# Attention scores of five groups in four 64x64 tiles over two PSUM banks, with a newly computed instruction order

## The chip, the cores and the metric

The kernel runs on one core of one Trainium2 chip. The metric is the device time of one execution in microseconds (us). Three runs of the kernel before gave 615.8, 616.06 and 616.22, so the median is 616.06 us.

## The reference

The reference chains three layers over 1152 tokens (2 batches of 576) of width 512 (8 heads of 64):

```python
scores = scale * np.matmul(q, k.transpose(0, 1, 3, 2))       # scale = 1/8
mask_local = (rel >= 0) & (rel < 32)                         # heads 0 to 3
mask_strided = (rel >= 0) & (pos[None, :] % 32 == pos[:, None] % 32)   # heads 4 to 7
attn = exp(scores - max) / (sum + 1e-09)
x = attn @ v                                                 # 1152 x 512
h = np.maximum(x @ w_in, 0.0); x = (h * h) @ w_out           # d_ff 2048
out += p[:, e:e+1] * (np.maximum(x @ w1[e], 0) @ w2[e])      # 4 experts of 1024, p = normalised domain_probs
```

All inputs are fp32.

## The kernel before, in words

**Attention.** Only the unmasked parts of the score matrix are computed, in 16 groups. A `Local` group is a window of queries of heads 0 to 3 (64 queries against 96 keys for a unit), a `Strided` group is a set of residues modulo 32 of heads 4 to 7 (54 or 36 rows for a unit). `attend` (L518 on) adds the steps of one group: three loads (k, q, v), the scores on TensorE (`scores`, L417 and L488), the mask, the row maximum on VectorE (`L556`), exp on ScalarE (`L561` or `L567`), the sum, the normalisation (`L571`), the transposes on TensorE (`L430`, `L501`), a copy to SBUF (`pt`, `L540`/`L542`), the product with v on TensorE (`L442`, `L511`) and the split of its result into a rounded and a rest part (`hi` `L582`/`L584`, `lo` `L588`). The scores are fp32 products of 64x64 tiles: head 0 of a unit uses array rows 0 to 63 and output partitions 0 to 63, head 1 rows 64 to 127 and partitions 64 to 127, all into one PSUM bank `S`. Each product is recorded in the trace as two matmuls (two passes).

The mask of -8e9 is added in one of two ways, group by group (`ON_PE`, for the ten groups after the first six). With 1, TensorE multiplies an identity by the mask first (`L421`, `L492`) and the scores accumulate on it. With 0, VectorE adds the mask while it copies the scores to SBUF (`L549`).

**First layer pair.** `run_steps` multiplies x by w_in (`H` in the banks `bh`, L774 to L776: three products for each split fp32 one), squares the ReLU (relu `L839` on ScalarE, square `L843` on VectorE, then `L846` and `L849` split the result into `h`), and multiplies by w_out two steps later (`by<-h,w`, also L774 to L776). The weights are loaded as 8-byte words, decoded (`L734`, `L737`, `L742`) and split (`L749`/`L751` and `L755`). From about 100 us on the same work goes through Strassen's scheme, and from about 250 us on the experts follow in a scheme of fifteen products.

**What sets the order.** Every step is a task of the class `Plan` with a cost in ns on each engine that may run it, a rank, PSUM or SBUF buffers that it takes and gives back, and the tasks that it follows. `Plan.run` plays the tasks through an event queue: an idle engine gets the ready task of the lowest rank whose buffers are free. The instructions are then emitted in that order, engine by engine, and the chip keeps it. Ranks and lead times are a table of numbers (`START` to `T_LEAD1`). Until the first product of the first layer is planned, an idle TensorE gets a filler product into a spare bank (`L1455`, 512 columns).

Of the kernel before, what the change touches and what calls it, by code (L numbers as in the profile page):

```python
# [68 lines left out]
class Plan:  # L69
# [33 lines left out]

    def run(self):
# [21 lines left out]
        while done < len(self.tasks):  # L126
# [25 lines left out]
            for e in ready:  # L152
                while idle[e] and ready[e]:
                    held, got = [], None
                    while ready[e]:
# [4 lines left out]
                        if not (t.quiet and e in self.tense or (t.port or e == "pool") and now < self.shared) and all(any(self.rings[r] for r in rings) for _, _, rings in t.take):  # L160
                            got = t
                            break
# [12 lines left out]
                    got.end = now + got.engines[e] * (2 if e == "pe" and now < self.warm else 1)  # L175
# [19 lines left out]
def tile_attention_mlp_experts(ctx: ExitStack, tc: tile.TileContext, a, out):  # L195
# [24 lines left out]
    HOLD = 4828  # L220
    AHEAD = 9478
    END2 = 25419
    END3 = -2590
    CONV = 19315
    CONV1 = 64257
    CONV2 = -317
# [3 lines left out]
    R_MASK = 1005  # L230
    ON_PE = (1, 1, 1, 1, 0, 0, 0, 0, 0, 0)
    FILL = 0
    R_MAX = -1769
    R_EXP = -5627
    R_NORM = 2220
# [3 lines left out]
    R_LO = -53571  # L239
    R_OUT = 2681  # L240
    FIRST = (-22394, 16695, 607, 23035, 8563, 1593)
    WHOLE = (1, 1, 1, 0, 0, 0)
    S_T, S_V, S_X = -14699, 658, 1170
    L_T, L_V, L_X = 4928, -8176, -46841
    LKQ = (-8725, -8905, -8392, -8132, -7820, -7895)
    LV = (-8661, -8282, -6737, -7657, -6434, -5679)
    LW = {("wi", 0, 1): -8036, ("wi", 0, 0): -7136, ("wi", 1, 1): -5574, ("wo", 0, 0): -7535, ("wo", 0, 1): -7891, ("wi", 1, 0): -6538}
    EARLY = {("wi", 0, 1): -35560, ("wi", 0, 0): 15804, ("wi", 1, 1): 33114, ("wo", 0, 0): 44988, ("wo", 0, 1): -1604, ("wi", 1, 0): 21441}
    GROUP = 4
    AHEAD_H = 3  # L250
    EARLY_H = (8793, 10693, 10315, 12215), (-10835, -8935, 44549, 46449), (8730, 10630, 20923, 22823), (19925, 21825, 13108, 15008)
# [7 lines left out]
    LEAD = 3482  # L259
    L_CB = -10608  # L260
    L_ID = -8381
    WI1 = 1
# [4 lines left out]
    S_LEAD = -14791  # L267
    S_LEAD1 = 75203
    T_LEAD1 = 28673
# [114 lines left out]
    class Strided:  # L384
# [32 lines left out]
        def scores(self, env, masked):  # L417
            self.views(env)
            n, s = self.n, env["S"]
            if masked:  # L420
                nc.tensor.matmul(s[:, : U * n], lhsT=cmat("ident", P), rhs=spread(cmat(self.R, P), U), start=True, stop=False)  # L421
            for u in range(U):
                for h in range(2):
                    hd = slice(h * D, (h + 1) * D)
                    nc.tensor.matmul(s[h * D : h * D + n, u * n : (u + 1) * n], lhsT=env["q3"][hd, u, :], rhs=env["k3"][hd, u, :], start=not masked, stop=not masked or u == U - 1)
# [9 lines left out]
        def values(self, env):  # L435
            n = self.n
            for h in range(2):
                for g in range(GROUPS):
                    c, q = (h * GROUPS + g) * n, g * P + h * D
                    for k in range(2):  # L440
                        rows = slice(k * D, k * D + n)
# [13 lines left out]
    class Local:  # L455
# [32 lines left out]
        def scores(self, env, masked):  # L488
            self.views(env)
            units, s = self.units, env["S"]  # L490
            for key, u, v in self.masks() if masked else ():
                nc.tensor.matmul(s[:, u * WIN : v * WIN], lhsT=cmat("ident", P), rhs=spread(cmat(key, P), v - u), start=u == 0, stop=False)  # L492
            for u in range(units):
                j, t = divmod(u, 2)
                for h in range(2):
                    hd = slice(h * D, (h + 1) * D)
                    nc.tensor.matmul(s[hd, u * WIN : (u + 1) * WIN], lhsT=env["q3"][hd, u, :], rhs=env["k3"][hd, t, j * WQ : j * WQ + WIN], start=not masked, stop=not masked or u == units - 1)  # L497
# [8 lines left out]
        def values(self, env):  # L506
            for u in range(self.units):
                for h in range(2):
                    j, t = divmod(u, 2)
                    c = t * self.nq + j * WQ  # L510
                    nc.tensor.matmul(env["X"][h * D : (h + 1) * D, c : c + WQ], lhsT=env["v3"][:, 4 * j + 2 * t + h, :], rhs=env["pt"][:WIN, u * P + h * WQ : u * P + (h + 1) * WQ], start=True, stop=True)  # L511
# [8 lines left out]
    def attend(g, rank, rings, lead, early=None, whole=False, on_pe_=1):  # L520
# [24 lines left out]
        t = plan.add({"pe": g.cost_s - (0 if masked else mm_r(n))}, lambda e: g.scores(env, masked), after=[t_cb, t_go, *loads[:2], *(transposed[-3:-2] if len(rings) == 1 else [])], rank=rank, take=[(env, "S", rings)], free=[(env, "q"), (env, "k")])  # L545
# [363 lines left out]
    def strassen(t_in, left, right, ready, w_free, s_free, rank_pe):  # L909
# [17 lines left out]
        def at(key):  # L927
            return c[key][:, :TB]
# [616 lines left out]
```

## Time and profile before

| | before |
|---|---|
| median of three runs | 616.06 us |
| the profiled execution, its own time | 616.26 us |
| its span (first to last instruction) | 614.3 us |
| TensorE matmul busy | 608.9 us, 99% |
| VectorE / ScalarE / GpSimdE busy | 455.9 / 300.7 / 133.0 us |
| last matmul ends, last VectorE instruction begins | 610.96, 610.99 us |

The span is 1.96 us less than the profiled execution's time; what lies around the span is launch and end. A timeline row has the start, the length, the engine, the line, the operation, the tiles written and read, the shapes and the count; where rows of one line follow each other they are merged. Lengths of matmuls overlap, so the cost of a piece is read from its start to the start of the next piece.

### The profile page before, as it was taken

The numbers are of one execution on the slowest core, as the hardware profiler recorded it, in microseconds if no ns is written. First come the engines' busy times: TensorE is split into PE (matmuls) and PEld (weight loads), VectorE is DVE, ScalarE is ACT, GpSimd is POOL, SyncE is SP. The second block draws the span as 40 slices with busy tenths as digits, with TensorE's granted clock in tenths as the row PEclk, the third lists the DMA queues.
The fourth block names the chain that finished last, engine by engine and source line by source line (L and its number), as shares of the span: only waits on it lengthen the run. The fifth ranks groups of instructions, "written<-read, shape, count | busy, mean of one in ns | idle before, by whom it ended". The sixth has DMA issues, their size and how long they took to land.

```text
span 614.3 us, 10072 instructions
## 1 busy us (share of the span) xinstructions
PE 608.9 (99%) x3739; PEld 558.5 (91%) x3739; DVE 455.9 (74%) x899; ACT 300.7 (49%) x698; POOL 133.0 (22%) x156
## 2 busy tenths in 40 slices
PE   9999999999999999999999999999999999999997
PEld 5798999999999999998898989898998989898996
DVE  5798868984797984977666675868866676987654
ACT  3778774755464653665344544334344534344330
POOL 3422113500010201032032232313141322224000
PEclk9999999999999999999999999999999999999999
DMA  8987422232313100030110203020201202020012
GB/s 262 303 252 229 125 83 70 68 96 77 103 52 87 36 0 18 1 86 18 38 49 18 86 19 86 18 86 17 65 22 32 74 17 86 18 86 1 1 52 102
DMA packets 37440, 45.13 MB, mean 73 GB/s; under 512 B 4688, under 2 KB 26640, under 8 KB 37392
## 3 DMA queue, kind: packets, MB, share of 16 engines
q1 hardware_dynamic: 37392, 44.50, 24.4%
q8 instruction: 29, 0.48, 0.3%
q14 instruction: 19, 0.16, 0.1%
HBM read 42.13 MB, written 2.36 MB: 72 GB/s over the span
## 4 chain that ended last, share of the span: by engine, by line
PE 96%; DMA 2%; DVE 0%; SPq 0%; ACT 0%; issue 0%; ACTq 0%
PE bh L774 12%; PE bh L776 12%; PE bh L775 12%; PE by L1307 11%; PE by L1306 11%; PE by L1308 11%; PE by L774 5%; PE by L776 5%; PE by L775 5%; PE ba L774 4%; PE ba L776 4%; PE ba L775 3%; DMA raw<-in_wi_dram 1%; PE ba L497 1%; DMA q<-in_qs_dram 1%; PE ba L511 1%
## 5 line engine op out<-in xcount | busy, mean ns | idle before, releaser
L1259 DVE SCALAR_TENSOR_TENSOR acc<-by,pe,acc 128x512 f32<-128x512 f32 (+1 forms) x109 | 79.3, 742 | 24.3 <-PE by L1308 24.0
L774 PE MATMUL bh<-x,w 128*128 128x384 f32 x234 | 80.5, 344 | 0.0
L776 PE MATMUL bh<-x,w 128*128 128x384 f32 x234 | 78.4, 335 | 0.0
L775 PE MATMUL bh<-x,w 128*128 128x384 f32 x234 | 78.4, 335 | 0.0
L1204 POOL TENSOR_TENSOR sf<-raw,raw 128x256 f32<-128x256 f32 x40 | 32.3, 816 | 185.9 <-DMA raw<-in_w_dram 108.0
L1215 ACT ACTIVATE w<-sf 128x256 fp32r<-128x256 f32 x110 | 42.0, 406 | 35.8 <-POOL sf L1204 35.8
L1307 PE MATMUL by<-o,h 128*128 128x512 f32 (+1 forms) x134 | 52.3, 390 | 0.0
L1306 PE MATMUL by<-o,h 128*128 128x512 f32 (+1 forms) x134 | 52.0, 388 | 0.0
L1308 PE MATMUL by<-o,h 128*128 128x512 f32 (+1 forms) x134 | 51.7, 386 | 0.0
L774 PE MATMUL by<-h,w 128*128 128x384 f32 x152 | 51.4, 338 | 0.0
L776 PE MATMUL by<-h,w 128*128 128x384 f32 x152 | 50.8, 335 | 0.0
L775 PE MATMUL by<-h,w 128*128 128x384 f32 x152 | 50.8, 334 | 0.0
L774 PEld LDWEIGHTS bh<-x,w 128*128 128x128 f32 x234 | 43.9, 188 | 2.4 <-DVE r L1426 1.1
L775 PEld LDWEIGHTS bh<-x,w 128*128 128x128 f32 x234 | 44.0, 188 | 0.4
L776 PEld LDWEIGHTS bh<-x,w 128*128 128x128 f32 x234 | 43.9, 188 | 0.0
L1328 ACT ACTIVATE h<-r 128x384 fp32r<-128x384 f32 x26 | 13.7, 525 | 53.5 <-DVE r L1426 53.5
L1204 POOL TENSOR_TENSOR sf<-sf,raw 128x256 f32<-128x256 f32 x40 | 32.1, 813 | 29.0 <-DVE w L1223 28.9
L775 PE MATMUL bh<-w,w 128*128 128x384 f32 x110 | 36.9, 336 | 0.0
L776 PE MATMUL bh<-w,w 128*128 128x384 f32 x110 | 36.9, 335 | 0.0
L1426 DVE TENSOR_TENSOR r<-r,bh 128x384 f32<-128x384 f32 x50 | 27.5, 550 | 12.6 <-ACT r L1421 7.9
L774 PE MATMUL bh<-w,w 128*128 128x384 f32 x110 | 36.8, 335 | 0.0
L1236 ACT ACTIVATE o<-raw 128x512 fp32r<-128x512 f32 x30 | 18.8, 631 | 35.1 <-PE by L1308 34.7
(282 smaller groups left out, 1615.6 us busy)
## 6 DMA issues: line engine op xcount, KB each, us to landing
raw<-in_wi_dram SPq DMA_DIRECT2D x16, 512.0 KB, 4.2
raw<-in_wo_dram SPq DMA_DIRECT2D x16, 512.0 KB, 4.5
raw<-in_w_dram SPq DMA_DIRECT2D x64, 128.0 KB, 2.7
raw<-in_w_dram SPq DMA_DIRECT2D x32, 256.0 KB, 2.8
out_dram<-acc SPq DMA_DIRECT2D x8, 256.0 KB, 2.0
v<-in_vs_dram SPq DMA_DIRECT2D x6, 256.0 KB, 5.1
v<-in_vl_dram SPq DMA_DIRECT2D x8, 192.0 KB, 5.6
k<-in_kl_dram SPq DMA_DIRECT2D x8, 160.0 KB, 4.6
```

What stands on the lines that cost most here:

```text
L774: nc.tensor.matmul(dst, lhsT=wh, rhs=xh, start=start, stop=False, skip_group_check=again)
L775: nc.tensor.matmul(dst, lhsT=wh, rhs=xl, start=False, stop=False, skip_group_check=again)
L776: nc.tensor.matmul(dst, lhsT=wl, rhs=xh, start=False, stop=stop, skip_group_check=again)
L1204: nc.gpsimd.tensor_tensor(out=value(dst), in0=value(x), in1=value(y), op=ALU.subtract if n in MINUS else ALU.add)
L1215: nc.scalar.activation(out=op_slot(env["op"])[:, 0].rearrange("p k f -> p (k f)"), in_=value(src), func=AF.Copy, scale=float(sign))
L1236: nc.scalar.activation(out=late[env["w2"]][:, 0], in_=f32(raws[f]["raw"][:, DM:]), func=AF.Copy)
L1259: nc.vector.scalar_tensor_tensor(out=acc, in0=o, scalar=pcol, in1=acc, op0=ALU.mult, op1=ALU.add)
L1306: nc.tensor.matmul(o, lhsT=h[:, 0, ts], rhs=w[:, 0], start=new, stop=False)
L1307: nc.tensor.matmul(o, lhsT=h[:, 0, ts], rhs=w[:, 1], start=False, stop=False)
L1308: nc.tensor.matmul(o, lhsT=h[:, 1, ts], rhs=w[:, 0], start=False, stop=stop)
L1328: nc.scalar.activation(out=got(env["hid"])[:, 0], in_=src(), func=AF.Relu)
L1426: nc.vector.tensor_tensor(out=at_(), in0=at_(), in1=bank["bank"][:, :TB], op=ALU.add if sign > 0 else ALU.subtract)
```

## The change

1. **Scores.** For groups with the mask on VectorE, the scores go to four tiles over two banks: unit u writes bank `S0` or `S1` by u modulo 2, and in odd units the two heads change places in the output partitions. So four neighbouring products have four different 64x64 tiles. The product with v reads its columns accordingly (`turned`). The second bank may be one of the pair `bank_h`, as may the one of the product with v (`HB`).
2. **Planned cost.** These scores are planned with 0.62 of the cost (`QUAD`). The planner checks that two buffers taken together are both free (`fits`), and it stretches or shortens planned DMA time by three factors.
3. **Mask and scale.** VectorE multiplies by the scale while it adds the mask, in one instruction for each bank and mask; the maximum comes out negated, so the later multiplication by -scale falls away for these groups.
4. **Which groups.** `ON_PE` goes from 1111000000 to 1110001001: five groups with the mask on VectorE instead of six.
5. **Squares.** In the first layer the square of a step may run on ScalarE (`SQ`). In the order that results, 21 of 32 do.
6. **The table.** Nearly every number of the table has another value, so the whole order of the first 250 us is another one.

```diff
-                        if not (...) and all(any(self.rings[r] for r in rings) for _, _, rings in t.take):
+                        if not (...) and self.fits(t):
...
-                    got.end = now + got.engines[e] * (2 if e == "pe" and now < self.warm else 1)
+                    slow = 2 if e == "pe" and now < self.warm else 1
+                    if e == "dma":
+                        slow = 1.25 if now < 5000 else 0.83 if now < 6700 else 1
+                    got.end = now + int(got.engines[e] * slow)
...
-    HOLD = 4828
+    HOLD = 5337
-    ON_PE = (1, 1, 1, 1, 0, 0, 0, 0, 0, 0)
+    SQ = (0, 50, 0)
+    QUAD = 0.62
+    HB = (1, 0, 1)
+    ON_PE = (1, 1, 1, 0, 0, 0, 1, 0, 0, 1)
...
                 for h in range(2):
-                    hd = slice(h * D, (h + 1) * D)
-                    nc.tensor.matmul(s[h * D : h * D + n, u * n : (u + 1) * n], lhsT=env["q3"][hd, u, :], ...)
+                    hd, c, y = slice(h * D, (h + 1) * D), h * D, s[:, u * n : (u + 1) * n]
+                    if not masked:
+                        c, y = (h + u) % 2 * D, env["S%d" % (u % 2)][:, u // 2 * n : (u // 2 + 1) * n]
+                    nc.tensor.matmul(y[c : c + n], lhsT=env["q3"][hd, u, :], ...)
...
+        more = rings if masked or not HB[0] else rings + ["bank_h"]
+        held = [(env, "S")] if masked else [(env, "S0"), (env, "S1")]
-        t = plan.add({"pe": g.cost_s - (0 if masked else mm_r(n))}, ..., take=[(env, "S", rings)], ...)
+        t = plan.add({"pe": g.cost_s if masked else int((g.cost_s - mm_r(n)) * QUAD)}, ..., take=[(x, y, rings if k == 0 else more) for k, (x, y) in enumerate(held)], ...)
...
-                    nc.vector.tensor_tensor(out=view(env["p"])[:, u:v], in0=view(env["S"], g.cols)[:, u:v], in1=spread(cmat(key, P), v - u), op=ALU.add)
+                    for k in range(2):
+                        x = env["S%d" % k][:, u // 2 * g.cols : v // 2 * g.cols].rearrange("p (u c) -> p u c", c=g.cols)
+                        nc.vector.scalar_tensor_tensor(out=pairs[:, k, u // 2 : v // 2], in0=x, scalar=SCALE, in1=spread(cmat(key, P), (v - u) // 2), op0=ALU.mult, op1=ALU.add)
...
-                    nc.vector.scalar_tensor_tensor(out=h, in0=h, scalar=0.0, in1=env["r"], op0=ALU.max, op1=ALU.mult)
+                    if e == "act":
+                        nc.scalar.activation(out=h, in_=env["r"], func=AF.Square, scale=WSCALE**0.5)
+                    else:
+                        nc.vector.scalar_tensor_tensor(out=h, in0=h, scalar=0.0, in1=env["r"], op0=ALU.max, op1=ALU.mult)
```

The order on TensorE, at the scores of a Strided group with 54 rows (k and q are its inputs, `ba` and `bh` PSUM banks, cb the mask). Before:

```order
L421 LDWEIGHTS cb
L421 MATMUL ba_106<-cb 128x432
L425 MATMUL ba_106<-k_116,q_112 54x54 x16
L442 MATMUL ba_105<-pt_130,v_122 64x54 x16
L774 MATMUL by_107<-h_97,w_82 128x384
```

Now, the group that follows it:

```order
L442 MATMUL ba_106<-k_115,q_111 54x54 x2
L442 MATMUL bh_104<-k_115,q_111 54x54 x2
L442 MATMUL ba_106<-k_115,q_111 54x54 x2
L442 MATMUL bh_104<-k_115,q_111 54x54 x2
L442 MATMUL ba_106<-k_115,q_111 54x54 x2
L442 MATMUL bh_104<-k_115,q_111 54x54 x2
L442 MATMUL ba_106<-k_115,q_111 54x54 x2
L442 MATMUL bh_104<-k_115,q_111 54x54 x2
L800 MATMUL by_107<-h_97,w_81 128x384
```

The mask product is gone for this group, and two banks alternate. It also shows that the first output product (`by_107<-h_97`) has moved: it follows this group's scores directly.

The order on TensorE, ahead of the first product of the first layer (`bh_103<-x_75,w_80`). Before:

```order
L501 MATMUL by_107<-ident,p_129 96x128 x4
L501 MATMUL ba_106<-ident,p_128 96x128 x4
L1455 LDWEIGHTS idle
L1455 MATMUL by_110<-idle 128x512
L1455 LDWEIGHTS idle
L1455 MATMUL by_110<-idle 128x512
L774 MATMUL bh_103<-x_75,w_80 128x384
```

Now:

```order
L459 MATMUL by_109<-pt_131,v_119 64x54 x16
L459 MATMUL ba_105<-pt_130,v_121 64x36 x16
L520 MATMUL ba_106<-ident,p_129 96x128 x4
L530 MATMUL by_107<-pt_131,v_123 64x64 x8
L800 MATMUL bh_103<-x_75,w_80 128x384
```

A product with v of a Local group now stands ahead of it, and no filler directly ahead. In the whole order there are 17 fillers in place of 23: 13, 3 and 1 in place of 9, 6, 4, 2 and 2.

The order on VectorE around the last preparation (`w_82` before, `w_81` now, both the second half of the first w_out unit) that the first output product needs. Before:

```order
L742 SCALAR_TENSOR_TENSOR val_95<-raw_91,val_95 128x512
L843 SCALAR_TENSOR_TENSOR bh_104<-bh_104,r_101 128x384
L568 TENSOR_REDUCE st_135<-p_129 128x8
L755 TENSOR_TENSOR w_82<-val_95,w_82 128x512
L849 TENSOR_TENSOR h_97<-bh_104,h_97 128x384
```

Now:

```order
L872 SCALAR_TENSOR_TENSOR bh_104<-bh_104,r_101 128x384
L768 SCALAR_TENSOR_TENSOR val_96<-raw_90,val_96 128x512
L594 TENSOR_REDUCE st_133<-p_126 128x8
L878 TENSOR_TENSOR h_97<-bh_104,h_97 128x384
L595 TENSOR_SCALAR st_133<-st_133 128x8
L781 TENSOR_TENSOR w_81<-val_96,w_81 128x512
```

Both stand as the 70th instruction of VectorE.

## Rows read from the trace of the kernel before

**Rows 1.** The page: span, and busy time of TensorE.

```profile
span 614.3 us, 10072 instructions
PE 608.9 (99%) x3739; PEld 558.5 (91%) x3739; DVE 455.9 (74%) x899; ACT 300.7 (49%) x698; POOL 133.0 (22%) x156
```

**Rows 2.** Waits of TensorE: engine, line, releaser: us in total, times, longest.

```profile
PE ba L425 <- DMA q<-in_qs_dram: 0.4, 2, 0.3
PE ba L442 <- DVE st L569: 0.4, 1, 0.4
```

**Rows 3.** Timeline of TensorE, 0 to 22 us: start, length, line, tiles, shapes, count.

```profile
0.99 4.02 PE L1455 MATMUL by<-idle 128*128 128x512 bf16 x9 [0.99 <-DVE idle L1459]
4.80 0.57 PE L421 MATMUL ba<-cb 128*128 128x432 bf16 x1
5.30 1.48 PE L425 MATMUL ba<-k,q 64*54 64x54 f32 x32
...
9.41 1.47 PE L1455 MATMUL by<-idle 128*128 128x512 bf16 x6
10.72 0.33 PE L492 MATMUL ba<-cb 128*128 128x192 bf16 x2
...
21.34 0.52 PE L774 MATMUL bh<-x,w 128*128 128x384 f32 x1
```

**Rows 4.** Timeline of VectorE: first row maximum, last rest part before 21.34 us.

```profile
6.83 0.61 DVE L556 TENSOR_REDUCE st<-ba 128x8 f32<-128x432 f32 x1 [5.89 <-PE ba L425]
...
20.99 0.35 DVE L588 TENSOR_TENSOR x<-ba,x 128x192 fp32r<-128x192 f32 x1
```

**Rows 5.** Timeline of TensorE: scores in two tiles, and the piece after each.

```profile
38.96 1.01 PE L425 MATMUL ba<-k,q 64*54 64x54 f32 x32
39.80 1.10 PE L442 MATMUL ba<-pt,v 54*64 54x54 f32 x32
...
43.12 0.75 PE L425 MATMUL ba<-k,q 64*36 64x36 f32 x32
43.80 0.44 PE L774 MATMUL by<-h,w 128*128 128x384 f32 x1
...
46.52 0.88 PE L497 MATMUL ba<-k,q 64*64 64x96 f32 x16
47.24 1.09 PE L442 MATMUL ba<-pt,v 54*64 54x54 f32 x32
```

**Rows 6.** Timeline of TensorE: the last product with v (column tiles), and its follower.

```profile
97.27 0.69 PE L511 MATMUL ba<-pt,v 96*64 96x64 f32 x16
97.88 0.44 PE L774 MATMUL bh<-x,w 128*128 128x384 f32 x1
```

**Rows 7.** Timeline of TensorE: masks of 384, 192 and 432 columns.

```profile
23.30 0.34 PE L492 MATMUL ba<-cb 128*128 128x384 bf16 x1
...
28.89 0.24 PE L492 MATMUL ba<-cb 128*128 128x192 bf16 x1
...
38.69 0.35 PE L421 MATMUL ba<-cb 128*128 128x432 bf16 x1
```

**Rows 8.** Timeline of TensorE: the first output products, after a small piece.

```profile
40.83 0.44 PE L774 MATMUL by<-h,w 128*128 128x384 f32 x1
41.11 0.34 PE L775 MATMUL by<-h,w 128*128 128x384 f32 x1
41.29 0.34 PE L776 MATMUL by<-h,w 128*128 128x384 f32 x1
```

**Rows 9.** Timeline of VectorE: the 70th instruction.

```profile
34.31 0.69 DVE L755 TENSOR_TENSOR w<-val,w 128x512 fp32r<-128x512 f32 x1
```

**Rows 10.** Busy time by stretch: length, PE, PEld, DVE, ACT, POOL, clock, DMA, GB/s.

```profile
6.83:21.34 14.51, 13.66 (x248) 10.48 (x248) 12.90 (x43) 9.01 (x34) 5.11 (x5) 1.00 1.02 290
20.00:40.00 20.00, 19.73 (x248) 16.31 (x246) 16.98 (x44) 15.73 (x45) 6.49 (x7) 1.00 0.98 307
40.00:60.00 20.00, 20.00 (x258) 18.23 (x255) 17.97 (x51) 14.57 (x40) 4.72 (x5) 1.00 0.75 210
```

More of the change, by code (lines that the diff above doesn't have):

```diff
@@ L102, in add, with fits @@
         return t
+    def fits(self, t):
+        used = {}
+        for _, _, rings in t.take:
+            r = next((r for r in rings if len(self.rings[r]) > used.get(r, 0)), None)
+            if r is None:
+                return False
+            used[r] = used.get(r, 0) + 1
+        return True
     def run(self):
@@ L159, in run @@
                             continue
-                        if not (t.quiet and e in self.tense or (t.port or e == "pool") and now < self.shared) and all(any(self.rings[r] for r in rings) for _, _, rings in t.take):
+                        if not (t.quiet and e in self.tense or (t.port or e == "pool") and now < self.shared) and self.fits(t):
                             got = t
@@ L489, in scores @@
             self.views(env)
[L490 removed]
+            units, s = self.units, env["S" if masked else "S0"]
             for key, u, v in self.masks() if masked else ():
@@ L495, in scores @@
                 for h in range(2):
-                    hd = slice(h * D, (h + 1) * D)
-                    nc.tensor.matmul(s[hd, u * WIN : (u + 1) * WIN], lhsT=env["q3"][hd, u, :], rhs=env["k3"][hd, t, j * WQ : j * WQ + WIN], start=not masked, stop=not masked or u == units - 1)
+                    hd, c, y = slice(h * D, (h + 1) * D), h * D, s[:, u * WIN : (u + 1) * WIN]
+                    if not masked:
+                        c, y = (h + u) % 2 * D, env["S%d" % (u % 2)][:, u // 2 * WIN : (u // 2 + 1) * WIN]
+                    nc.tensor.matmul(y[c : c + WQ], lhsT=env["q3"][hd, u, :], rhs=env["k3"][hd, t, j * WQ : j * WQ + WIN], start=not masked, stop=not masked or u == units - 1)
         def transposes(self, env):
@@ L600, in tile_attention_mlp_experts @@
     for k, g in enumerate(second):
-        attend(g, START - AHEAD + k * (due(half) - START - END2) // len(second), ["bank_a"], LEAD, on_pe_=ON_PE[k])
+        attend(g, START - AHEAD + k * (due(half) - START - END2) // len(second), ["bank_a"], LEAD, whole=g.units > 4, on_pe_=ON_PE[k])
     third = [Local(1, j) for j in (2, 3, 4)]
@@ L925, in on_dve, with on_both @@
             return plan.add({"dve": dve(TB)}, emit, after=after, rank=t_in - 5 * URGENT + turn, **more)
+        def on_both(emit, after, turn=0, **more):
+            return plan.add({"act": act(TB), "dve": dve(TB)}, emit, after=after, rank=t_in - 5 * URGENT + turn, **more)
         def at(key):
```

101 lines of the change are left out of this document (53 added, 48 removed).

## The prediction

> **What bounds the kernel.** I read the page first: TensorE is busy for 608.9 of 614.3 us [rows 1]. The waits of TensorE come next, since a chain through one full engine can only be shortened by less work on it or fewer holes. The two largest after the initial memset are 0.4 us each [rows 2]. So from the first product of the first layer, at 21.34 us [rows 3], to the end, TensorE runs almost without a hole, and the other engines' time is cover. What moves the end is (a) TensorE work added or taken away, (b) how much real work is done when that first product can start, and (c) new holes. The third view is the timeline of the start, where the holes are filled: 23 fillers in the order, 9 ahead of the first mask at 4.80 us [rows 3] and 14 after it. A filler is no work: fewer of them save time only if something useful starts earlier.
>
> The sum is made against the profiled execution, 616.26 us; the median of the runs is 0.2 lower. A change of 0.2% (1.23 us) is about what a measurement of this kernel can tell from none.
>
> **Scores in four tiles.** Now, in two tiles, a 54-row group takes 39.80 - 38.96 = 0.84 us, a 36-row group 43.80 - 43.12 = 0.68, and a Local group of four units 47.24 - 46.52 = 0.72 [rows 5]. The five changed groups are one, one and three of these: 0.84 + 0.68 + 3 x 0.72 = 3.68 us. If four tiles ran side by side as freely as two, this would halve, a gain of 1.84. If the second pair of tiles adds nothing, the gain is 0. Costlier than two tiles it should not get: the count of passes is the same, and switching between banks is already done, between neighbouring pieces, without a visible gap. For a value between these ends I go by the nearest row. Two tiles of one set of array rows (the column tiles of a product with v) take 97.88 - 97.27 = 0.61 us for 16 passes of 64 columns [rows 6], two tiles of different rows 0.72 for 16 of 96 [rows 5]; both kinds of neighbour overlap today, and four tiles need both at once. That speaks for the upper end; against it speaks that no row shows three tiles at work. I take 0.6 of the gain: **-1.1 us, between -1.8 and 0.**
>
> Against this stands one mechanism. The order has 16 products for a 54-row group where the trace has 32 matmuls: each product is two passes on one tile. If TensorE starts matmuls strictly in order, the second pass of a product waits for its first, nothing behind it may start, and only the second pass of one product and the first of the next overlap. This gives two at work whatever the number of tiles, and the same 0.72 us. The Trainium skill, "TensorE: Matmul & The Clock Gate", Part 3 (packing small matmuls), states that order: matmuls start and end strictly in program order. By that rule the term is 0 in place of -1.1. The rows fit both readings, so it is a rival below.
>
> **Masks.** TensorE loses one mask of 432 columns and gains one of 384 and one of 192: 0.34 + 0.24 - 0.35 = **+0.2 us** [rows 7].
>
> **Fewer stretches of small pieces.** The first big product after small pieces starts its successor after 41.11 - 40.83 = 0.28 us, the next after 41.29 - 41.11 = 0.18 [rows 8]: 0.1 us for each return, and the first small product loses about as much. Counted in the order from the first layer's first product to the last product with v, there are 23 stretches of small pieces before and 20 now: 3 x 0.15 = **-0.4 us**, between -0.5 and 0.
>
> **The start.** Nine fillers take 0.42 us each (4.80 - 0.99 over 9), six later ones 0.22 each (10.72 - 9.41 over 6) [rows 3]: the first ones run at half the pace. Thirteen first fillers instead of nine move the first mask by 4 x 0.42 = 1.7 us at the half pace, less if the last run at the full one: 6.1 to 6.5 us instead of 4.80. In return the first group runs at the full pace: its mask took 5.30 - 4.80 = 0.50 us and its scores 1.48 [rows 3]; at full pace these are 38.96 - 38.69 = 0.27 [rows 5, 7] and 1.01 [rows 5]. So VectorE gets its first scores 0.6 to 1.0 us later than at 6.83 [rows 4]. The first product of the first layer is released when VectorE ends a rest part at 20.99 + 0.35 = 21.34 us [rows 4], the very start of that product. VectorE's list ahead of it grows by one normalisation and one copy and loses a weight copy and a shift, about 0.1 to 0.2 us more; its own holes ahead of it, 14.51 - 12.90 = 1.6 us [rows 10], can take up some of the delay. So that product begins at 21.2 to 22.4 us, and I take 21.65. By then TensorE has done one more product with v, 0.61 us of work [rows 6]. Net -0.3 us, between -0.8 and +0.5. Six fillers less are thus hidden: what they filled was waiting for VectorE, which stays.
>
> **What hides the rest.** The mask on VectorE becomes 12 shorter instructions for seven, the multiplication by -scale goes, and 21 squares move to ScalarE, whose busy time is 15.73 of 20 us at its fullest against VectorE's 17.97 [rows 10]. All of this is off TensorE's path: **0**, as long as each product of the first layer has its weights and `h` in time. The order says where that becomes narrow. Ahead of the first output product there are now 24 big products instead of 48 after the first one: 24 x 0.18 = 4.3 us less, and by the order some 2 us fewer small pieces. So TensorE is there at about 40.83 - 6.3 = 34.5 us [rows 8] and needs VectorE's 70th instruction. That one ended at 34.31 + 0.69 = 35.0 us [rows 9]. Before, it was 40.83 - 35.0 = 5.8 us early; now it may be late by 0.5, and more if VectorE falls behind. The two waits of 0.4 us [rows 2] may go or be replaced. For new and old holes together I take **0**, between -0.7 and +2.
>
> The sum: -1.1 + 0.2 - 0.4 - 0.3 + 0 = -1.6; 616.26 - 1.6 - 0.2 = **614.5 us** on the scale of the median. The tail after the last matmul is the same in both orders: the last ten instructions of VectorE are alike.
>
> **Rivals.**
>
> *Passes in order: four tiles give nothing.* For it: the fit to the two-tile rows. Against it: nothing in the trace. Then the sum is +0.2 - 0.4 - 0.3 = -0.5, or 615.6 us. Chance 0.22.
>
> *VectorE becomes the bound between 30 and 80 us: slower.* The last product with v moves from 97.27 us [rows 6] to about 79 by the work that the order puts ahead of it (an estimate), so the same softmax work is squeezed into a shorter stretch, while VectorE has only 20.00 - 16.98 = 3.0 and 20.00 - 17.97 = 2.0 us free in 20 to 40 and 40 to 60 us [rows 10]. Some eight squares leave this stretch; two Local groups come into it. If VectorE falls behind, each of the next weight units arrives late on TensorE; with four such places of 0.9 us, about double the 0.4 us of the waits seen now [rows 2], +3.6 on the forecast: about 618. It decides once the sum of holes passes 1.6 us. Against it: the order keeps output products two steps behind. Chance 0.19.
>
> *The start and the tiles both give all.* If VectorE's holes take up the whole delay and the six fillers were real holes, the start gives -1.3 instead of -0.3, and the tiles -1.8: 616.26 - 0.2 - 1.8 + 0.2 - 0.4 - 1.3 = 612.8 us. Chance 0.17.
>
> That the change doesn't do what it says is small as a rival: the order shows alternating banks in all five groups.
>
> **From the cases to the numbers.** The forecast has 0.42, with a range of its own of 613.7 to 615.6. Faster by over 0.2% means below 614.83: three quarters of the forecast (0.32), the fast rival (0.17) and a little of the first (0.02), 0.51. Slower means above 617.29: nearly the whole slow rival and what lies beyond, 0.20. The rest is 0.29. The range from 612.6 to 617.6 reaches over the fast rival and to the beginning of the slow one.
>
> **What would show it.** Scores of the five groups at 0.45 to 0.6 us for 0.72 and 0.84 show the tiles at work; 0.7 and 0.84 show passes in order. The first layer's first product at 21.2 to 22.4 us shows the start right; below 21, the fast rival. Waits of TensorE beyond 1.5 us between 22 and 80 us, released by VectorE or by a weight's preparation, show the slow rival. A time difference that arises after 250 us would mean that I looked at the wrong place, since the work is the same there.

## The result, and the profile after

The changed kernel takes 619.36 us in the median of 8 runs (617.48 to 621.97), the kernel before 616.03 (8 runs). The ratio is 1.0058, with a 95% interval from 1.0041 to 1.0075: slower, where 614.5 was forecast, and outside the range that was given.

The page of the profiled execution (621.36 us), span and busy times:

```profile
span 619.4 us, 10047 instructions
PE 609.6 (98%) x3734; PEld 558.4 (90%) x3734; DVE 446.1 (72%) x884; ACT 311.1 (50%) x721; POOL 124.8 (20%) x150
```

The span is 5.1 us longer than before [rows 1], TensorE's busy time only 0.7 us. So 4.4 us are stops of TensorE. The waits of TensorE, where before the two largest after the memset were 0.4 us each [rows 2]:

```profile
PE ba L436 <- DMA cb<-in_cb_dram: 1.0, 1, 1.0
PE by L1489 <- DVE idle L1493: 1.0, 1, 1.0
PE bh L800 <- DVE h L878: 0.9, 2, 0.5
PE bh L530 <- DVE h L878: 0.8, 1, 0.8
PE ba L516 <- DMA q<-in_ql_dram: 0.6, 1, 0.6
PE ba L442 <- ACT pt L559: 0.6, 1, 0.6
PE by L459 <- ACT pt L559: 0.5, 1, 0.5
PE ba L520 <- POOL p L597: 0.4, 1, 0.4
```

TensorE's busy time hides a second loss. The busy time by stretch (length; PE, PEld, DVE, ACT, POOL; granted clock; DMA share; GB/s) around the first product of the first layer:

```profile
16.00:20.60 4.60, 3.96 (x82) 3.30 (x77) 3.61 (x13) 3.39 (x12) 0.30 (x1) 1.00 1.06 268
20.60:22.00 1.40, 0.98 (x10) 0.69 (x6) 1.04 (x5) 1.28 (x3) 1.40 (x2) 0.58 1.11 277
22.00:26.00 4.00, 4.00 (x27) 3.05 (x27) 2.75 (x9) 2.25 (x5) 1.46 (x2) 0.50 1.03 295
26.00:28.00 2.00, 2.00 (x21) 1.77 (x20) 0.56 (x1) 0.00 (x0) 0.00 (x0) 0.59 0.95 338
```

After several stops between 18 and 21.2 us the granted clock falls to 0.50, the level of 1.2 GHz (full is 2.4), and stays there until after 27 us. The timeline of TensorE in that stretch shows the stops and the price, 0.32 us from one product to the next (23.74 to 24.06) where it was 0.18 [rows 8]. A bracket gives the engine's idle time before the row and what ended it:

```profile
18.35 1.14 PE L459 MATMUL by<-pt,v 54*64 54x54 f32 x32 [0.49 <-ACT pt L559]
...
21.18 1.09 PE L520 MATMUL ba<-ident,p 128*96 128x128 f32 x4 [0.42 <-POOL p L597]
...
23.25 0.69 PE L800 MATMUL bh<-x,w 128*128 128x384 f32 x1
23.74 0.52 PE L801 MATMUL bh<-x,w 128*128 128x384 f32 x1
24.06 0.52 PE L802 MATMUL bh<-x,w 128*128 128x384 f32 x1
```

The first product of the first layer begins at 23.25 us, against 21.34 before [rows 3]. The scores in four tiles, on the other hand, do what was hoped. The first Local group takes 44.86 - 44.37 = 0.49 us where two tiles took 0.72 [rows 5], the second 0.50, the third gains less and takes 70.80 - 69.71 - 0.42 = 0.67 us without the stop behind it:

```profile
44.37 0.56 PE L516 MATMUL ba<-k,q 64*64 64x96 f32 x16
44.86 0.44 PE L800 MATMUL by<-h,w 128*128 128x384 f32 x1
...
69.71 0.66 PE L516 MATMUL ba<-k,q 64*64 64x96 f32 x16
70.80 0.44 PE L800 MATMUL bh<-x,w 128*128 128x384 f32 x1 [0.42 <-DVE h L878]
```

The 54-row group takes 36.87 - 36.28 = 0.59 us for 0.84, the 36-row group 41.55 - 41.07 = 0.48 for 0.68.

The changed kernel ran in three series (here and below), 19 runs, which I split by the mean granted clock of the run. Eight runs have 0.999 or more (called full clock below): 617.13 to 619.49 us, median 617.96. Eleven have 0.997 or less: 618.87 to 621.97, median 619.67. So at full clock the change costs about 1.9 us, and a fall of the clock, in more than half of the runs, about 1.7 us on top. The two groups overlap.

### The profile page after: what moved, and what is told of

It reads as the page before. It is cut to its first block, busy times and chain, and to the rows that moved or that the text cites. A ratio compares the mean times of both kernels' runs of the same rounds, so it can differ in the third digit from the quotient of the medians.

```text
span 619.4 us, 10047 instructions
## 1 busy us (share of the span) xinstructions
PE 609.6 (98%) x3734; PEld 558.4 (90%) x3734; DVE 446.1 (72%) x884; ACT 311.1 (50%) x721; POOL 124.8 (20%) x150
## 4 chain that ended last, share of the span: by engine, by line
PE 94%; DMA 2%; DVE 1%; ACT 1%; issue 1%; SPq 0%; POOL 0%; POOLq 0%; ACTq 0%
PE bh L800 12%; PE bh L802 11%; PE bh L801 11%; PE by L1341 11%; PE by L1340 11%; PE by L1342 11%; PE by L800 5%; PE by L801 4%; PE by L802 4%; PE ba L800 4%; PE ba L802 3%; PE ba L801 3%; DMA raw<-in_wi_dram 1%; PE ba L516 1%; DMA cb<-in_cb_dram 1%
## 5 line engine op out<-in xcount | busy, mean ns | idle before, releaser
L800 PE MATMUL bh<-x,w 128*128 128x384 f32 x238 | 82.3, 346 | 0.9 <-DVE h L878 0.9
L802 PE MATMUL bh<-x,w 128*128 128x384 f32 x238 | 80.2, 337 | 0.0
L801 PE MATMUL bh<-x,w 128*128 128x384 f32 x238 | 80.2, 337 | 0.0
L1238 POOL TENSOR_TENSOR sf<-raw,raw 128x256 f32<-128x256 f32 x40 | 34.0, 859 | 189.4 <-DMA raw<-in_w_dram 122.3
L1341 PE MATMUL by<-o,h 128*128 128x512 f32 (+1 forms) x131 | 51.1, 390 | 0.0
L1340 PE MATMUL by<-o,h 128*128 128x512 f32 (+1 forms) x131 | 50.9, 388 | 0.0
L1342 PE MATMUL by<-o,h 128*128 128x512 f32 (+1 forms) x131 | 50.6, 386 | 0.0
L800 PEld LDWEIGHTS bh<-x,w 128*128 128x128 f32 x238 | 44.9, 189 | 3.9 <-DVE h L878 1.6
L801 PEld LDWEIGHTS bh<-x,w 128*128 128x128 f32 x238 | 45.0, 189 | 0.4
L802 PEld LDWEIGHTS bh<-x,w 128*128 128x128 f32 x238 | 45.0, 189 | 0.0
L1255 DVE TENSOR_TENSOR w<-sf,w 128x256 fp32r<-128x256 f32 x80 | 33.2, 427 | 7.6 <-ACT w L1249 4.7
```

Of the source, the lines that this page charges most:

```text
L800: nc.tensor.matmul(dst, lhsT=wh, rhs=xh, start=start, stop=False, skip_group_check=again)
L801: nc.tensor.matmul(dst, lhsT=wh, rhs=xl, start=False, stop=False, skip_group_check=again)
L802: nc.tensor.matmul(dst, lhsT=wl, rhs=xh, start=False, stop=stop, skip_group_check=again)
L1238: nc.gpsimd.tensor_tensor(out=value(dst), in0=value(x), in1=value(y), op=ALU.subtract if n in MINUS else ALU.add)
L1255: eng[e].tensor_tensor(out=l, in0=value(src), in1=f32(h), op=ALU.subtract)
L1340: nc.tensor.matmul(o, lhsT=h[:, 0, ts], rhs=w[:, 0], start=new, stop=False)
```

## The experiments

### The tiles

**two_tiles.** Both banks stay, the turning of the heads goes (in the scores of both kinds of group, and in the product with v that reads them):

```diff
-    c, y = (h + u) % 2 * D, env["S%d" % (u % 2)][...]
+    c, y = h * D, env["S%d" % (u % 2)][...]
```

> The changed kernel with the heads of odd units no longer turned: the five groups still write two banks by turns and everything else stays where it is, but neighbouring products lie in two 64x64 tiles instead of four. Theory (the four tiles give the gain): the scores of these groups go back from 0.59, 0.48 and 0.49 us to about 0.84, 0.68 and 0.72 us. Rival (the second bank or the missing mask gives it): they stay at 0.48 to 0.59 us.

One run, 618.72 us at clock 1.000. The timeline of TensorE:

```profile
41.05 0.88 PE L516 MATMUL ba<-k,q 64*64 64x96 f32 x16
41.86 0.44 PE L800 MATMUL by<-h,w 128*128 128x384 f32 x1
```

0.81 us at the place where four tiles took 0.49. The 54-row group takes 33.27 - 32.34 = 0.93:

```profile
32.34 0.31 PE L442 MATMUL ba<-k,q 64*54 64x54 f32 x4 [0.48 <-ACT pt L559]
32.48 0.27 PE L442 MATMUL bh<-k,q 64*54 64x54 f32 x4
...
33.27 0.44 PE L800 MATMUL by<-h,w 128*128 128x384 f32 x1
```

In four tiles it takes 33.19 - 32.64 = 0.55 us, here in the profile of cb_first (below):

```profile
32.64 0.26 PE L442 MATMUL ba<-k,q 64*54 64x54 f32 x2 [0.48 <-ACT pt L559]
32.65 0.26 PE L442 MATMUL bh<-k,q 64*54 64x54 f32 x2
32.73 0.22 PE L442 MATMUL ba<-k,q 64*54 64x54 f32 x2
32.74 0.22 PE L442 MATMUL bh<-k,q 64*54 64x54 f32 x2
...
33.19 0.44 PE L800 MATMUL by<-h,w 128*128 128x384 f32 x1
```

Same banks, same order, same missing mask: the four tiles alone make the scores short. If a second pass held back everything behind it, there would be no difference, so that rival falls. The rows show it too: two records of bank ba are followed by two of bh before the other two of ba, where two tiles give four and four.

The time can't tell the two kernels apart: 618.72 lies among the runs of the changed kernel at full clock. And the late stops of the changed order (their own part stands below) are here too, with 0.48, 0.78, 0.23 and 0.45 us. So slow scores do not remove them.

**tiles_alone.** The code of the change with the old table: old start, old loads, squares on VectorE, no factors on DMA times. The order is planned from it. Some of the lines:

```diff
-    HOLD = 5337
+    HOLD = 4828
...
-    SQ = (0, 50, 0)
+    SQ = (0, 0, 0)
...
-    ON_PE = (1, 1, 1, 0, 0, 0, 1, 0, 0, 1)
+    ON_PE = (1, 1, 1, 1, 0, 0, 0, 0, 0, 0)
...
-    L_CB = -11160
+    L_CB = -10608
```

> The code of the change with the numbers of the table before (its start, its loads in the old order, squares on VectorE, no stretched DMA times): six groups with four tiles, the order otherwise nearly that of before. Theory (four tiles give 0.2 to 0.25 us a group, and the loss of the changed kernel comes from the new order alone): 616.0 - 1.2 = 614.8 us, between 614.3 and 615.3, clock 1.000. Rival (the tiles give nothing on the end, since VectorE's extra instructions or the pair of banks take it back): 616.0 or above.

618.24 us (5 runs, all at clock 1.000), ratio 1.0037 (1.0025 to 1.0049): slower than before although nothing of the start was changed. My theory, that the loss lay in the new order of the table alone, fell here. The timeline of TensorE has two large stops that before did not have (and two of 0.20 and 0.36 us at 46.56 and 47.32 us):

```profile
62.33 0.45 PE L800 MATMUL bh<-x,w 128*128 128x384 f32 x1 [1.11 <-DVE p L574]
...
76.01 0.44 PE L800 MATMUL bh<-x,w 128*128 128x384 f32 x1 [1.20 <-DVE h L878]
```

At 62.33 a product of the first layer waits for bank bh, which the scores had borrowed as their second bank, until VectorE has read it for the mask (L574). At 76.01 it waits for bh until the rest part (L878) has read it. My reading is that shorter scores bring TensorE sooner to a bank that VectorE and ScalarE have not yet released. It is not shown: VectorE's mask instructions and the lent bank are new here too, and no run takes one of the three alone.

**no_lending.** The same, and no bank bh for attention (`HB = (0, 0, 0)`); the order is planned anew.

> The kernel of tiles_alone (618.24 us) with both banks of a group's scores and of its product with v taken from the pair ba, none from the pair bh of the first layer's products; the order is planned anew. Theory (bh, lent to scores, comes back late and stops the next product of the first layer): the waits of bh products on VectorE (1.1 us for the mask, 1.2 us for the last rest part) go, and the time is 615 to 616.5 us. Rival (VectorE is late there whatever the bank): waits of 2 us or more stay between 45 and 90 us, at 618 us or above.

618.85 us, 1.0049 (1.0034 to 1.0064). The wait for the mask at bh is gone; 0.80 us for L878 (79.44 us), 0.59 for the mask at ba (47.53 us) and three of 0.25 to 0.37 us stand in its place. With the rival's 2 us of waits still there, lending is one way in which the lateness shows, not its cause.

### The late stops of the changed order

In every profile that keeps TensorE's changed order, whatever its start, the same four places stop TensorE: 0.48 us for ScalarE's copy pt (0.60 in the changed kernel's own profile), 0.78, 0.42 and 0.45 us for the release of a bank bh by L878, together 2.1 us. Here they are in cb_first (below), whose clock does not fall:

```profile
32.64 0.26 PE L442 MATMUL ba<-k,q 64*54 64x54 f32 x2 [0.48 <-ACT pt L559]
...
50.92 0.69 PE L530 MATMUL bh<-pt,v 96*64 96x64 f32 x16 [0.78 <-DVE h L878]
...
67.09 0.44 PE L800 MATMUL bh<-x,w 128*128 128x384 f32 x1 [0.42 <-DVE h L878]
...
79.88 0.44 PE L800 MATMUL bh<-x,w 128*128 128x384 f32 x1 [0.45 <-DVE h L878]
```

**no_low.** Which engine is behind? VectorE loses one instruction for each weight, so the kernel leaves out the lowest bits of the weights:

```diff
-    emit(e)
+    if emit.__name__ != "low":
+        emit(e)
```

> The changed kernel without the instruction on VectorE (L768, 0.68 us) that adds the lowest bits of a decoded weight of the first layer pair, left out for all 32 units, so the result is slightly less exact; nothing takes its place. Theory (VectorE is the bound between 30 and 90 us, and each of TensorE's waits there ends with it): the waits of TensorE between 30 and 90 us fall from 2.2 us to below 0.8, and the runs at full clock come down from 617.5 to about 616 us. Rival (ScalarE or the order is the bound): 1.5 us or more of these waits stay, 617 us or above.

617.81 us, 1.0029 (1.0019 to 1.0039). The stops of 0.48, 0.42 and 0.45 us stay to the hundredth, only 0.78 shrinks to 0.44, with a new one of 0.17 behind it. This is the rival's outcome (ScalarE or the order is the bound): VectorE's load is not what sets three of the four. In the profile of the changed kernel ScalarE's part (L875, which VectorE's L878 follows) ends at 70.16 us, L878 at 70.75, the stop at 70.80; L875 stood behind four exps there:

```profile
69.33 0.35 ACT L586 ACTIVATE p<-ba,st 128x96 f32<-128x96 f32 x1
...
69.65 0.51 ACT L875 ACTIVATE h<-bh 128x384 fp32r<-128x384 f32 x1
```

**sq_back.** The squares return to VectorE, at their planned places (`emit("dve" if emit.__name__ == "square" else e)`).

> The changed kernel with its 21 squares on ScalarE back on VectorE, each at its planned place; TensorE, GpSimd and the loads keep their order. Theory (VectorE is the bound there): TensorE's waits between 30 and 90 us grow by 1 us or more, 618.5 us or above at full clock. Rival (ScalarE, which now carries the squares, is the late one): the waits shrink and the time falls below 617.5 us.

618.79 us, 1.0053 (1.0036 to 1.007); 618.19 to 619.14 at full clock. The four stops stay (0.48, 0.78, 0.33, 0.51), and two of 0.20 and 0.39 us come in addition, at 63.82 and 216.23 us, both at L878. That is neither the theory's 1 us more nor the rival's shrinking. So the squares on ScalarE are no loss that these runs show, and the stops do not hang on the place of the squares.

**moved.** TensorE's order itself: four output products are put into two of the stops, task 50 ahead of the scores 49, tasks 109 to 111 ahead of the first-layer product 105.

```diff
+        ahead = {pe[a][1]: [pe[k] for k in ks] for a, ks in {49: [50], 105: [109, 110, 111]}.items()}
...
+            for _, _, emit, e in [*ahead.get(x[1], ()), *([] if x[1] in gone else [x])]:
```

> The changed kernel with four output products (3 matmuls each) moved on TensorE: one ahead of the scores that wait 0.5 us at 32 to 36 us, three ahead of the first-layer product that waits 0.42 us at 67 to 71 us. Theory (TensorE's order puts a product there whose bank is not free, while other work is ready): both waits go, 0.9 us less, 616.6 us at full clock. Rival (nothing else is ready there either, since VectorE and ScalarE are behind with weights and h): the waits move to the output products and the time stays within 0.3 us of the changed kernel's.

617.75 us, 1.003 (1.0019 to 1.004); at full clock 616.86 to 617.75, where the changed kernel on the same chip has 617.13 to 619.49 in six runs (two series). Four runs against six, with medians of 617.17 and 618.16: about the 0.9 us of the two stops, and within the spread. Both stops are gone from the timeline. The moved products lose 0.15 us at 31.70 us and 0.2 us at 65.96 us, where the second matmul starts 0.49 us after the first and not 0.28:

```profile
65.96 0.44 PE L800 MATMUL by<-h,w 128*128 128x384 f32 x1
66.45 0.44 PE L801 MATMUL by<-h,w 128*128 128x384 f32 x1
```

So work was ready that the order held back. For the other two stops the next output products cannot be taken: the rest part of their weights is written later in the order.

### The start

**cb_first.** The load of cb ahead of the four that precede it on SP's queue.

```diff
+        for _, _, emit, e in [x for x in rows if x[2] is self.soon] + [x for x in rows if x[2] is not self.soon]:
             emit(e)
...
+    plan.soon = t_cb.emit
```

> The changed kernel, with the load of the mask constants (cb) issued ahead of the four k and q loads that now precede it. Theory (late loads at the start make the holes): the wait of 1.0 us for cb goes, the first scores start up to 1.0 us earlier than 6.62 us, the first product of the first layer up to 1.0 us earlier than 23.25 us, and the time falls by 0.5 to 1.0 us to about 618.5; what remains of the holes from 17 to 22 us still lets the clock fall in part of the runs. Rival (k and q come later by the same amount): first scores at 6.3 us or later, and no change beyond 0.3 us.

618.08 us, 1.0046 (1.003 to 1.0062). The wait for cb goes, but the scores start at 7.03 us (6.62 before the edit), behind 13 fillers that now take 5.5 us: no gain, as the rival had it. The wait for q at 14.7 us is 0.78 us (0.61 before the edit, with 0.36 for another q). At full clock the runs lie at 617.26 to 619.69 us, as those of the changed kernel do. So late loads of cb cost nothing that shows. In this profile the first product of the first layer begins at 21.68 us, 0.03 from the forecast.

**before_no_fill.** The kernel before without its last 14 fillers, all else in place.

> The kernel before without its last 14 fillers (9 to 21.3 us); the order of all else is unchanged. Theory (holes at the start cost clock): the granted clock falls to 0.5 for some us between 10 and 28 us, and the time rises by 1 to 4 us above 616.0 with a spread over the runs. Rival (fillers only cover waits, as the prediction took them): granted clock 1.00, 616.0 us within 0.3.

616.50 us, 1.0004 (0.9995 to 1.0012). Seven of 11 runs have a clock of 0.997 or less, against one of 20 of the kernel before on the same chip. The busy time by stretch, with the stops and the fall behind them:

```profile
10.00:12.00 2.00, 0.88 (x16) 0.72 (x16) 2.00 (x8) 0.54 (x3) 0.30 (x1) 1.00 0.98 326
12.00:14.00 2.00, 1.69 (x9) 1.02 (x9) 2.00 (x8) 1.71 (x6) 1.16 (x2) 0.81 1.01 270
14.00:16.00 2.00, 2.00 (x29) 1.94 (x30) 1.42 (x4) 0.77 (x6) 1.51 (x2) 0.50 1.01 334
16.00:18.00 2.00, 2.00 (x37) 1.68 (x35) 0.73 (x5) 0.67 (x2) 0.49 (x1) 0.84 1.09 256
```

So a filler is more than cover: it keeps the clock. Here the fall costs little: the medians with and without it are 616.59 and 616.19 us, and the whole ratio is not clear of 1. My reading is that it lies ahead of the first layer, where TensorE has time to lose. In the changed kernel's profile it lay on the first layer's products.

**filled_holes.** The changed kernel with 11 fillers at the start.

> The changed kernel, with 11 more fillers put where TensorE stood still ahead of the first layer (4 before the first mask, 1 before the third Local group's mask, 2 each ahead of the places at 14.3, 18.35 and 21.2 us). Theory (TensorE's standing still lets the granted clock fall to 0.5 for some 6 us, worth up to 3 to 4 us, in part of the runs): the granted clock stays at 1.00 from 16 to 30 us in every run, the runs lie within 0.5 us of each other, at 617.5 us (as the two runs at clock 1.000 did). Rival (the clock falls for another reason, or the fillers delay real work by their 0.2 us each): runs spread over 2 us or more as now, median 619 us or above.

618.95 us, 1.006 (1.004 to 1.0079), 617.66 to 622.79: the stops of the start are gone from the profile, the spread is not. The expectation missed. One run has clock 0.994, and 0.78 us at 51.06 us still stands.

### What lets the clock fall

**after_again.** The changed kernel once more.

> The changed kernel itself, once more, beside its variants on one chip. Theory (its order alone costs about 1.5 us at full clock; the rest, up to 4 us, is a fall of the granted clock at the start that comes in part of the runs): runs at clock 0.999 or above lie at 617.3 to 618.3 us, runs below 0.998 at 619 to 622 us. Rival (the slower runs have another cause): runs at clock 0.999 or above reach 619.5 us or more too.

619.09 us, 1.0044 (1.003 to 1.0059); four of 6 runs at 0.997 (618.91 to 619.84), the others 617.13 and 618.11. The profile shows the fall in another place:

```profile
51.10 0.69 PE L530 MATMUL bh<-pt,v 96*64 96x64 f32 x16 [0.78 <-DVE h L878]
51.72 0.82 PE L516 MATMUL ba<-k,q 64*64 64x96 f32 x16
52.47 0.69 PE L800 MATMUL bh<-x,w 128*128 128x384 f32 x1
52.95 0.52 PE L801 MATMUL bh<-x,w 128*128 128x384 f32 x1
```

The granted clock is 0.50 in 52 to 54 us and back at 1.00 by 56. It follows the stop of 0.78 us. The profile of moved_decode (below) shows the same, 0.51 in 52 to 54 us behind its stop of 0.77 us at 50.92 us.

**late_fill.** Small fillers of 128 columns in the four late stops (8, 13, 7 and 7).

```diff
+        extra, count = {49: 8, 78: 13, 105: 7, 128: 7}, 0
...
+    plan.late = lambda e: nc.tensor.matmul(spare[:, TB:], lhsT=idle, rhs=idle, start=True, stop=True, ...)
```

In this kernel and the next two the output is off by a relative 0.21. My reading is that the fillers disturb the sums in the first 384 columns of the bank that they write to; no run separates this. The other instructions are the same, so I use these three kernels for their times and clocks alone.

> The changed kernel with small fillers (an identity-sized bf16 product of 128 columns into columns of a by bank that nothing uses) in the four stops of TensorE after 30 us: 8, 13, 7 and 7 of them; the start is as it was. Theory (a stop of TensorE of some tenths of a us lets the granted clock fall for some 3 us after it, wherever it lies; the stop of 0.78 us at 51 us is one): no run shows a half-level stretch after 30 us, runs below 0.998 become fewer than 4 in 6, and those left have theirs at the start; full-clock runs stay at 617.3 to 618.3 us. Rival (late stops have no part in it): runs at 0.997 as often as in after_again.

618.46 us, 1.0036 (1.0026 to 1.0046). One of 10 runs is at 0.997; the others reach 619.30 us, beyond the 618.3 expected.

**all_fill** has six old fillers at the start besides.

> The kernel of late_fill with 6 more of the old fillers at the start as well (1 before the mask at 10.8 us, 4 ahead of 13.4 us, 1 ahead of 20.2 us). Theory: granted clock 0.999 or above in every run, 617.2 to 618.3 us, no run above 619. Rival (the clock falls without stops too, or DMA at the start moves the runs): spread above 619 us with clock 0.999 or above, or clock below 0.998 in part of the runs.

618.33 us, 1.0033 (1.0022 to 1.0045), 617.91 to 618.77, all 6 runs at 0.999 or more.

**moved_fill** is moved with fillers in the two stops that it leaves.

> The kernel of moved (two of the four stops filled with real work) with small fillers in the two that are left (13 and 7). Theory: clock 0.999 or above in nearly all runs and a median of 617.0 us, 0.7 us below the moved kernel's 617.75 and 2 us below the changed kernel's. Rival: median 617.7 us or above with runs at 0.997 as before.

617.71 us, 1.0024 (1.0015 to 1.0033), none of 11 runs below 0.999. The median of 617.0 was not reached.

Together: with the stop of 0.78 us filled, 1 of 27 runs has a clock of 0.997 or less. With the stop in place (the three series of the changed kernel, cb_first, filled_holes, sq_back, two_tiles, moved, and the two of the next part), 24 of 57 have. no_low, whose stop is 0.44 us, has 0 of 10.

Two things weaken this. The share differs by chip: of the 57, the runs on one chip have 14 of 29, those on another 4 of 20 (the first series has 6 of 8). The filled kernels ran on a third chip, without an unfilled one beside them, and 1 of 27 against 4 of 20 could be chance, as could no_low's 0 of 10 on the chip with 4 of 20. And the size of a stop alone does not decide: tiles_alone, whose profile has stops of 1.11 and 1.20 us, has clock 1.000 in all 5 runs, and no_lending, with a stop of 0.80 us, has none of 4 below 0.999.

So that stops bring the clock down is shown by making them in before_no_fill, beside the kernel before on one chip. That the stop of 0.78 us does it in the changed order is seen in two profiles and fits the counts; it is not shown beyond that, and which stop did it in a run that was not profiled stays unknown.

### The spread at full clock

In the two profiles with a late first product, ScalarE waited 1.2 to 1.3 us for the first load of w_in, here in the changed kernel's, and the copy pt that TensorE needs stood behind it:

```profile
16.83 0.68 ACT L760 ACTIVATE mid<-raw 128x512 f32<-128x512 f32 x1 [1.19 <-DMA raw<-in_wi_dram]
```

**after_third** is the changed kernel on the same chip as the two that follow.

> The changed kernel once more, as the measure for decode_later on the same chip. Expected from its two series: full-clock runs (0.999 or above) between 617.1 and 618.5 us, runs below 0.998 at 618.9 to 622 us, these in more than half of the runs.

618.84 us, 1.0044 (1.0032 to 1.0056); four runs at full clock, 617.71 to 619.49, one at 0.997. The run of 619.49 at full clock is what after_again's rival named: the clock does not explain all slow runs.

**decode_later.** The decode moves behind the copies.

```diff
-        for _, _, emit, e in sorted(order, key=lambda x: x[:2]):
+        rows = sorted(order, key=lambda x: x[:2])
+        rows = rows[:77] + rows[78:87] + [rows[88], rows[77], rows[87]] + rows[89:]   # 77: small, 87: shift
```

> The changed kernel with the first decode of a weight (ScalarE L760 and VectorE L763) moved behind the copies of two transposes (L559, L561) that now stand behind it. Theory (in some runs the first load of w_in lands late, ScalarE waits up to 1.3 us for it, and the copies, TensorE's next products and the first product of the first layer come that much later): TensorE's waits for pt at 18.3 us go, the first product of the first layer begins at 21.0 to 21.7 us, and the spread at full clock shrinks to 617.0 to 617.9 us; runs below 0.998 stay, after the 0.78 us stop. Rival (the spread has another source): full-clock runs up to 619 us as in late_fill.

619.24 us, 1.0063 (1.0047 to 1.008); full clock 617.93 to 618.86. The wait is gone from the profile (first product at 21.56 us), no gain is seen, and three of 6 runs still lose clock. **moved_decode** joins it with moved.

> The kernel of moved with the edit of decode_later: the changed order with two of its four late stops filled by work and without the wait for the first load. Theory: full-clock runs at 616.3 to 617.0 us, a median of 616.8 us, 2 us below the changed kernel and 0.7 us above the kernel before. Rival: median 617.7 us as in moved.

618.91 us, 1.0045 (1.0033 to 1.0057), three of 5 runs below 0.998, the two at full clock 617.82 and 617.92. This theory fell: the late load explains a late start where a profile shows it, not the spread of the series. What makes runs at full clock differ by 2 us stays open.

### Other tables

**new_numbers** and **new_numbers_b** keep the start of before and place the rest anew, with five and six groups in four tiles (the expectation below says seven; `ON_PE` has six zeros).

> The code of the change with another table: the start, the first six groups and their loads as in the kernel before (23 or so fillers, cb first), five Local groups with four tiles (mask on VectorE), squares on either engine, and new ranks for the rest that leave fewer planned stops of TensorE between 30 and 90 us. Theory (the tiles pay where the order leaves no new holes and the start keeps its clock): waits after 22 us below 1 us, clock 1.000, 616.0 - 0.9 = 615.1 us, between 614.4 and 615.7. Rival (with the shorter scores VectorE and ScalarE cannot keep up in any order): waits of 1.5 us or more between 30 and 90 us, 616.0 us or above.

> As new_numbers, with a second table found from another start: seven groups with four tiles, squares of steps 9 to 16 on either engine. Theory: 615.2 us, between 614.4 and 615.9, the tiles giving 0.3 us more and the masks on VectorE more to hide. Rival: 616.0 us or above, with holes released by VectorE.

617.00 us, 1.0021 (1.0012 to 1.003): no stop after 30 us, but 0.84, 0.82 and 0.97 us between 18 and 30, released by VectorE, a load of q and VectorE, and 0.90 us at 7.68 for a load of q. And 616.32 us, 1.0008 (0.9999 to 1.0016): stops of 0.21 to 0.45 us only, clock 0.999 or more in 10 of 11 runs, as fast as before but not faster. No version here beats the kernel before.

## Why the prediction was wrong

The step that failed is **"What hides the rest ... For new and old holes together I take 0, between -0.7 and +2"**. In cb_first, at full clock, TensorE is busy for 608.1 us, 0.8 less than before, and the span is 615.8 us. So the holes, the span less the busy time, are 7.7 us where before they were 5.4: +2.3 in place of 0. Of this, 2.1 us are the four late stops, which stand in every profile that keeps the order; before had 0.15 us after its first product of the first layer. The slow rival had the stretch (30 to 80 us) right, though at 0.9 us each it overpriced its places; that they were four is luck, since it only supposed a number. It named VectorE as the bound and late weight units as the place. The runs showed banks in place of weights: a product waits for a bank that ScalarE alone (the first stop), or ScalarE and VectorE one after the other, have not released. I looked at the weights' instruction alone (VectorE's 70th; the stop there came from ScalarE's copy), and at busy shares, which say nothing of a chain through both engines. Why the banks come back late is not isolated: two_tiles keeps the stops with slow scores, moved removes two of them by order alone, so they belong to the order more than to the shorter scores.

The second failure is a term that the sum did not have: the **granted clock**. I took fillers as cover ("six fillers less are thus hidden"). They are, but what they also keep off is a fall of the clock by half, for some 3 and 6 us in two profiles above. No row of the kernel before shows such a fall: its granted clock is 1.00 in all stretches of [rows 10].

The other terms:

- **Scores in four tiles, -1.1:** right. Against the durations of [rows 5] the five groups gain 0.25 + 0.20 + 0.23 + 0.22 + 0.05 = 0.95 us in the changed kernel's profile. The Trainium skill, "TensorE: Matmul & The Clock Gate", Part 3, states that matmuls start and end strictly in program order. For the two passes of a fp32 product the trace differs: in the rows of cb_first above, two records of bank bh start at 32.65 us, ahead of the second two of ba at 32.73 us. The 0 of the rival needed more than that rule, namely that a second pass holds back the products behind it, and this is not borne out: products in four tiles took 0.49 us where the same products in two tiles took 0.81.
- **The start, -0.3:** first mask at 6.34 us (6.1 to 6.5 forecast), first product of the first layer at 21.3 to 21.9 us in 12 of the 14 profiles of the changed order (21.65 forecast), 22.5 and 23.25 in the two others. The order of the loads on SP, where cb went from the first place to the fifth, I did not read; cb_first shows no cost of it by itself. In cb_first the 17 fillers take as long as the 23 did (6.6 and 6.7 us from their starts to the next), since 13 of them run at half pace, 5.52 us.
- **Fewer stretches, -0.4:** not found. Summed over the first 100 us, from each matmul's start to the next, kernel before and cb_first: scores 12.7 and 11.7 us, transposes 6.3 and 8.2, products with v 12.4 and 12.6, masks 3.4 and 3.9 (stops are counted with the matmul ahead of them). Without their stops the transposes grew by 0.7 us, the products with v shrank by 0.1, and the big products took 0.2 longer over the whole span (568.3 against 568.1). Why the transposes grew stays open.
- **Masks, +0.2:** 0.1 in these sums without the stops.

## What to carry to other kernels

When the order on a full engine changes, or it gets faster at something, look at who must give back what it reuses next: follow each PSUM bank from the last product into it to the last read of it, over all engines, and compare that with the order's distance to the next use. Price each new stop of TensorE twice, once as the stop and once as the chance that its clock falls after it. A filler in a stop can keep the clock, but it does not give the stop's time back (all_fill, all at full clock, takes 618.33 us, the changed kernel at full clock 617.96). A table of numbers that re-orders everything needs its own forecast: here the tiles were worth about 1 us, and what came with them cost more than twice that.

## Not expected of the hardware

- The granted clock falls to 0.50 for about 3 us after one stop of 0.78 us in a TensorE that is busy for 9.83 of the 10 us before it, in part of the runs, at the same place of the same program (after_again). tiles_alone, whose profile has stops of 1.11 and 1.20 us, shows no fall in any of 5 runs.
- Two heads that change places make 16 passes of 96 columns take 0.49 instead of 0.81 us. Two banks without that change bring nothing: 0.81 us stands beside 0.72 [rows 5] to 0.80 us for one bank in the kernel before, here 71.41 - 70.61:

```profile
70.61 0.88 PE L497 MATMUL ba<-k,q 64*64 64x96 f32 x16
71.41 0.69 PE L511 MATMUL ba<-pt,v 96*64 96x64 f32 x16
```

- With filler products in columns 384 to 511 of a bank whose columns 0 to 383 hold sums, the output is off by a relative 0.21, though the fillers write none of these columns. That they disturb the sums there is my reading; no run separates it.
